# Channel product: upper remainders stacked over lower ones, with a new written order

## The chip, the cores and the metric

The kernel runs on one core of a Trainium2 chip. It uses TensorE (PE, its weight loads PEld), VectorE (DVE), ScalarE (ACT), GpSimd (POOL) and the SyncE queue (SP), from which the loads and stores are issued; transfers inside the core's memory are issued from POOL. The metric is the device time of one execution in microseconds. Before the change three timed runs gave 355.57 to 356.24 us, median 355.92.

## The reference

Two stages, one after the other. The first is a gated linear attention with a running state, over 4 batches, 8 heads, 768 tokens and head size 40:

```python
m_new = np.maximum(f_gate[:, :, t] + m, i_gate[:, :, t])
f_stab = np.exp(f_gate[:, :, t] + m - m_new)
i_stab = np.exp(i_gate[:, :, t] - m_new)
C = f_stab * C + i_stab * np.einsum('bhd,bhe->bhde', vt, kt)
n = f_stab * n + i_stab * kt
y = sigmoid(o_gate) * (C @ qt) / np.maximum(np.abs(n . qt), 1.0)
```

The second works on its result x, laid out as 4 batches x 768 tokens x 320 channels:

```python
theta = x @ w_theta
zr, zi = x * np.cos(theta), x * np.sin(theta)
y = einsum('ts,bsd->btd', w_tok_r, zr) + einsum('ts,bsd->btd', w_tok_i, zi)
u = x + y
out = u + np.maximum(u @ w_ch, 0.0)
```

The last line is the channel product. Weights arrive as 64-bit words and are decoded on the chip.

## The kernel before

Tokens are cut into 6 chunks of 128. A unit is one chunk of one batch: 24 units, numbered n = 4 * chunk + batch. Two batches make a pair `pr` (0 or 1); 12 pairs q = n // 2. A unit runs on TensorE as scores (`score`, L370), the products of weighted scores with the values (`pv`, L406 and L410) and a state product (`state`, L454). ACT makes the exponentials (`exps`, L389), POOL cuts them to a triangle (`select`, L393), and DVE multiplies them into the scores (`weigh`, L399; below, the unit's weighting). A unit's denominator (L417 to L424), its output gate (L430 or L432) and `head_out` (L439) give its part of X.

For each pair of units X is turned (L609), split into an upper part rounded to the fast 32-bit format and a lower remainder (L621, L625), and multiplied by `w_theta` (`angles`, L647). The angles are reduced (L655 to L671), sine and cosine are taken on ACT (L674, L675), multiplied by X (L684) and split into upper and lower parts of z (L687, L690). Five groups j of the token mix (L549, 12 products each for a pair and a chunk) add into `acc` (`gather`, L563). The token weights are decoded in 18 pieces of 512 columns (`split`, L263 to L285); four operations of a piece (L269 to L271, L275) run on DVE only, the others may go to ACT, DVE or POOL.

Every product of two such numbers takes three matmuls: upper by upper, lower weight by upper, upper weight by lower. The channel product (`channel`, L944 to L956) has 320 rows of contraction for a batch, 128 + 128 + 64. The two batches of a pair lie one behind the other in five tiles of 128 rows, so tile 2 holds the last 64 rows of the first batch in its upper half of partitions, and the first 64 rows of the second in its lower half. Output tiles jj = 0, 1 belong to the first batch, 3, 4 to the second, 2 to both. `ks_of` (L930) lists the parts of an output tile. They run in blocks of half the tokens (384 columns): a pair block for (0, 3) or (1, 4), and a single block for 2. In a pair block, 18 matmuls, the three half products of jj and the three of jj + 3 take turns, on the two halves of the partitions:

```python
products = [*x[:6], *(z for xy in zip(x[6:], y[:3]) for z in xy), *y[3:]]
```

There are 8 pair blocks of 18 matmuls and 4 single blocks of 15. The parts of u are `us[pr, k]`, upper and lower side by side, written by `u_hi` (L922) and `u_lo` (L925). The channel weights are decoded into two tiles, upper in `E_.w[0]` and lower in `E_.w[1]`, and rows that belong on the other half of the partitions are copied there by eight POOL transfers (`wch_copies`, L905). ReLU and sum are one DVE operation (`relu`, L967), then the store (L177).

What is computed is collected by `add` as numbered tasks with the engines that may run them; `issue` (L125) issues them in the order of `ORDER` (L47), a list written out by hand such as `934T`: task 934, on TensorE. V is DVE, A ACT, G POOL, D SP's loads and stores. Each engine works its tasks strictly in this order. Priorities and estimated times given to `add` play no part any more. The tasks 961 to 1028 are filling products on `ones` (L878), which keep TensorE busy; with a V behind their number they do nothing.

Of the kernel before, what the change touches and what calls it, by code (L numbers as in the profile page):

```python
# [10 lines left out]
F32R = mybir.dt.float32r  # L11
# [8 lines left out]
P = 128  # L20
# [13 lines left out]
WCOLS = 1792  # L34
PIECE = 512
# [17 lines left out]
117V 220V 108A 109A 173T 256D 161V 221V 162V 222A 230D 110V 239D 163A 118V 113G 174V 120T 223G 255D 225A 164V 111A
243G 175T 121V 180A 122V 980V 226V 240T 123A 231A 112V 124A 983T 227V 181T 176A 114A 232V 228A 305D 119A 370D 250A
254D 177V 115V 125V 135T 178V 260A 306D 182V 128G 179V 241V 183T 129V 244V 229G 233V 245T 371A 130V 184A 376D 372V
257D 186A 138A 251T 137A 234A 185V 261G 258T 126A 246V 136V 310A 324D 247V 323D 127V 131T 373V 235V 382D 304D 248A
259V 322D 147T 262V 318G 311G 374A 249V 133A 252A 263T 268V 963V 148V 375G 377A 132V 253V 134A 149A 378V 307D 150A
383A 187T 264A 328A 390D 384V 269T 188A 379V 308T 265V 270A 522D 189V 329G 985T 380A 312V 388D 190A 143T 309G 302D
191A 266V 381G 267V 271V 313T 385V 523A 192V 394A 524V 326T 408D 139T 314V 406D 525V 325D 315V 330V 395G 316A 389D
528D 144V 392T 140V 526V 193A 195V 145A 319T 194G 146A 396V 196A 272T 407D 142A 534D 410T 386A 456D 197V 141A 273A  # L60
988V 320V 214T 327V 412A 317V 387G 275V 321V 527G 331T 529A 215V 391D 274V 336A 530V 276T 458D 338A 474D 332V 999V
216V 989V 971V 333V 217A 531V 334G 337T 277A 393G 198T 335V 535A 457D 339V 413G 462A 278V 409D 536V 397T 532A 964V
279V 303A 974V 414V 463G 202T 476D 402G 674D 199V 200V 398V 201V 280A 411V 206T 399V 537V 204V 400G 203V 205V 460T
404A 281V 968V 284V 282A 210T 540D 208V 283G 454D 285A 992V 997V 464V 209A 680D 480A 403T 286V 478T 207V 533G 405V
401V 340T 459D 212V 415T 538V 211V 213V 675A 481G 341V 420A 990V 343V 539G 293T 342V 542D 416A 558D 676V 344T 482V
417V 1010V 294V 418G 546A 295V 544T 345V 290T 677V 461V 686D 678A 475D 346V 547G 422A 419V 421T 681A 679G 291V 347A
299T 292V 348A 682V 424T 301V 465T 470V 488A 548V 349G 300V 352G 423V 425A 562T 466V 687A 477D 426V 472A 287T 683V
353A 541D 467V 350A 427V 354G 455A 471T 970V 289V 428T 351G 473V 288V 543D 468V 479V 361T 995V 469V 559D 429A 560D
1007V 688V 684A 483T 554V 430V 545G 363V 431A 572G 965V 367T 484V 362V 564A 610D 485V 608D 490V 626D 975V 689V 489T
# [8 lines left out]
767G 764T 1021V 1002V 780D 836A 713D 585V 702A 644T 768V 588G 516T 844D 645A 761D 1025V 703V 589V 704A 707T 1012V
1011V 647V 782T 646V 779D 586A 590V 648T 587V 715G 705V 518V 969V 708G 719T 649V 517V 650V 1014V 841V 651A 600T 1027V
720V 709V 652A 721V 763D 967V 722A 653V 603T 602V 656G 601V 784A 846D 1018V 723V 758D 591T 605V 858D 726V 604V 765V  # L80
728T 593V 769T 592V 657A 785G 731V 774A 729V 837G 725T 658G 776A 597T 727V 654A 792G 759A 770V 730V 781D 655G 732T
# [964 lines left out]
```

## Time and profile before

| | before |
|---|---|
| timed runs, median (lowest to highest) | 355.92 us (355.57 to 356.24) |
| profiled execution, its own time | 357.73 us |
| its span, first to last instruction | 356.0 us |
| mean granted TensorE clock | 0.947 |
| PE, DVE, ACT, POOL busy | 325.5, 297.3, 220.5, 123.1 us |
| matmuls | 2286 |
| moved by DMA | 61.56 MB |

Busy time is the time in which at least one instruction of the engine was running; matmuls overlap, so a matmul's own duration is longer than the step from one to the next. The granted clock is 1.0 or 0.5 at any moment. "Idle before" a group names what released its first instruction.

### The profile page before, as it was taken

The numbers are of one execution on the slowest core, as the hardware profiler recorded it, in microseconds if no ns is written. First come the engines' busy times: TensorE is split into PE (matmuls) and PEld (weight loads), VectorE is DVE, ScalarE is ACT, GpSimd is POOL, SyncE is SP. The second block draws the span as 40 slices with busy tenths as digits, with TensorE's granted clock in tenths as the row PEclk, the third lists the DMA queues.
The fourth block names the chain that finished last, engine by engine and source line by source line (L and its number), as shares of the span: only waits on it lengthen the run. The fifth ranks groups of instructions, "written<-read, shape, count | busy, mean of one in ns | idle before, by whom it ended". The sixth has DMA issues, their size and how long they took to land.

```text
span 356.0 us, 6570 instructions
## 1 busy us (share of the span) xinstructions
PE 325.5 (91%) x2286; PEld 303.9 (85%) x2289; DVE 297.3 (84%) x629; ACT 220.5 (62%) x567; POOL 123.1 (35%) x111
## 2 busy tenths in 40 slices
PE   1487969979899999998999999999999999999995
PEld 1366959859799999997999989999999989998885
DVE  4998699786889998999989998798899998658632
ACT  2989788888979979596585838987850412201000
POOL 1223442323434636247352611614330092702000
PEclk9877676978999999999899999999999999999999
DMA  6965792996886764489627286346630021000155
GB/s 228 395 228 172 226 261 57 302 327 214 244 329 215 243 210 134 152 250 323 203 71 257 79 263 238 121 142 193 228 87 0 2 43 33 1 2 0 46 196 202
DMA packets 25164, 61.56 MB, mean 173 GB/s; under 512 B 3204, under 2 KB 11052, under 8 KB 25132
## 3 DMA queue, kind: packets, MB, share of 16 engines
q1 hardware_dynamic: 23915, 59.84, 51.1%
q0 software_dynamic: 1216, 1.31, 2.0%
q8 instruction: 18, 0.29, 0.3%
q14 instruction: 15, 0.11, 0.1%
HBM read 55.71 MB, written 4.12 MB: 168 GB/s over the span
## 4 chain that ended last, share of the span: by engine, by line
PE 63%; DVE 17%; DMA 12%; ACT 3%; POOL 2%; issue 2%; SPq 2%; DVEq 0%; POOLq 0%
PE pm L549 25%; PE pm L955 10%; PE pm L647 9%; PE ph L410 8%; DMA qk<-in_qk 5%; DMA eb<-e_d 4%; PE sc L370 3%; PE ph L406 3%; DVE acc L563 2%; PE pm L454 2%; DVE dt L399 2%; DMA q_t<-in_q 2%; DMA sg<-in_og 1%; DVE val L271 1%; DVE val L275 1%
## 5 line engine op out<-in xcount | busy, mean ns | idle before, releaser
L549 PE MATMUL pm<-w,z 128*128 128x384 f32 x600 | 112.2, 339 | 0.0
L549 PEld LDWEIGHTS pm<-w,z 128*128 128x128 f32 x600 | 103.4, 188 | 1.4 <-DVE acc L563 0.2
L563 DVE TENSOR_TENSOR acc<-pm,acc 128x384 f32<-128x384 f32 x100 | 52.1, 549 | 10.9 <-PE pm L549 10.6
L389 ACT ACTIVATE dt<-dt,bwT 128x128 f32<-128x128 f32 x160 | 49.0, 391 | 7.7 <-DMA dt<-g_d 7.6
L410 PE MATMUL ph<-tok_t,dt 128*128 128x41 f32 x384 | 49.4, 291 | 0.0
L410 PEld LDWEIGHTS ph<-tok_t,dt 128*128 128x128 f32 x384 | 48.5, 205 | 0.7 <-issue 0.2
L393 POOL TENSOR_SCALAR_AFFINE_SELECT dt<-dt 128x1024 f32<-128x1024 f32 (+1 forms) x26 | 29.3, 1130 | 49.6 <-ACT dt L389 37.5
L647 PE MATMUL pm<-wthp,xs 128*128 128x320 f32 (+1 forms) x216 | 38.3, 352 | 3.2 <-DVE xs L625 3.2
L647 PEld LDWEIGHTS pm<-wthp,xs 128*128 128x128 f32 (+1 forms) x216 | 30.7, 206 | 8.7 <-issue 4.8
L399 DVE TENSOR_TENSOR dt<-sc,dt 128x512 f32<-128x512 f32 x44 | 28.1, 680 | 1.4 <-PE sc L370 1.3
L955 PE MATMUL pm<-u,w 128*128 128x384 f32 (+1 forms) x112 | 28.4, 355 | 0.0
L370 PE MATMUL sc<-qk 64*128 64x128 f32 x352 | 26.5, 292 | 1.8 <-DMA qk<-in_qk 1.8
L370 PEld LDWEIGHTS sc<-qk 64*128 64x128 f32 x352 | 22.2, 193 | 5.2 <-issue 1.6
L690 POOL TENSOR_TENSOR z<-ab,z 128x640 fp32r<-128x640 f32 x8 | 12.8, 1603 | 35.8 <-DVE den L423 21.4
L549 PE MATMUL pm<-wsm,z 128*128 128x384 f32 x120 | 24.6, 359 | 0.0
L967 DVE SCALAR_TENSOR_TENSOR acc<-pm,acc 128x384 f32<-128x384 f32 x20 | 10.8, 555 | 14.5 <-PE pm L955 14.5
L549 PEld LDWEIGHTS pm<-wsm,z 128*128 128x128 f32 x120 | 22.2, 201 | 0.2
L406 PE MATMUL ph<-C,q_t 120*128 120x123 f32 x120 | 17.2, 279 | 5.2 <-DVE X L439 2.7
L406 PEld LDWEIGHTS ph<-C,q_t 120*128 120x128 f32 x120 | 15.4, 191 | 6.8 <-POOL q_t L484 3.0
L955 PEld LDWEIGHTS pm<-u,w 128*128 128x128 f32 (+1 forms) x112 | 17.6, 187 | 3.0 <-issue 3.0
L430 ACT ACTIVATE sg<-sg,den 128x40 f32<-128x40 f32 x72 | 16.7, 314 | 5.0 <-DVE den L424 5.0
L922 ACT CAST u<-acc 128x768 fp32r<-128x768 f32 x4 | 3.2, 834 | 26.4 <-DVE acc L563 21.5
(136 smaller groups left out, 603.8 us busy)
## 6 DMA issues: line engine op xcount, KB each, us to landing
qk<-in_qk SPq DMA_DIRECT2D x24, 512.0 KB
dt<-g_d SPq DMA_DIRECT2D x20, 512.0 KB
raw<-in_wtok SPq DMA_DIRECT2D x18, 512.0 KB
tok_t<-in_tok SPq DMA_DIRECT2D x24, 364.5 KB
sg<-in_og SPq DMA_DIRECT2D x12, 320.0 KB
q_t<-in_q SPq DMA_DIRECT2D x20, 180.0 KB
eb<-e_d SPq DMA_DIRECT2D x60, 60.0 KB
out<-acc SPq DMA_DIRECT2D x5, 384.0 KB
```

The source lines that it names most:

```text
L370: nc.tensor.matmul(u.sc[s][:, hp], u.qk[rows, 1, hp], u.qk[rows, 0, hp], start=True, stop=True)
L389: nc.scalar.activation(u.dt[:, h, :], src, AF.Exp, bias=bwT[:, c, r:r + 1])
L393: nc.gpsimd.affine_select(d, d, pattern=[[0, h1 - h0], [1, P]], compare_op=ALU.is_ge, fill=0.0, base=0, channel_multiplier=-1)
L399: nc.vector.tensor_mul(d2[:, s], u.sc[s], d2[:, s])
L406: nc.tensor.matmul(u.ph[:, gg * 3 * E1:(gg + 1) * 3 * E1], u.q3[:, gg, :], C[b][:, gg, :], start=(gg == 0), stop=False)
L410: nc.tensor.matmul(u.ph[:, h * E1:(h + 1) * E1], u.dt[:, i, :], v1(h, h + 1), start=(c == 0 and i == 0), stop=(i == H - 1))
L430: nc.scalar.mul(u.s3[:, h], u.s3[:, h], u.den[:, h])
L549: nc.tensor.matmul(pm[:, :TH], x.z[:, a, s, j * P:(j + 1) * P], w[x.c][:, b, s, th * TH:(th + 1) * TH], start=(k == 0), stop=(k == last))
L563: nc.vector.tensor_add(a, pm[:, :TH], a)
L647: nc.tensor.matmul(S_.th[b - b0][:, :DM], p.xs[a0:a1, a, k, :], wt5[a0:a1, s, k, :], start=(x == of(b)[0]), stop=(x == of(b)[-1]))
L690: ENG[e].tensor_sub(zv(1, s), trig(s), zv(0, s).bitcast(F32))
L955: nc.tensor.matmul(o.pm[jj][:, :TH], E_.w[s][a0:a1, col:col + P], us[pr, k][a0:a1, a, ts], start=(x == ones[jj][0]), stop=(x == ones[jj][-1]))
```

## The change

A new tile `both` is laid over `wt5`, the `w_theta` tile, which is free after the last angles. For each pair it holds, for the 64 remainder rows of either batch, the upper part of u on one half of the partitions and the lower part of the same rows on the other half. `hi_again` writes the upper parts from `acc` (two copies of 64x768, on DVE in the new order), `lo_across` moves the lower parts across (two POOL transfers). `wch_twice` places the upper weights of these rows, 256 columns, on both halves, in 512 more columns of `E_.w[0]` (four POOL transfers). One matmul over 128 rows of `both` then does upper by upper and upper weight by lower together. The lower weight by upper stays a 64-row matmul; the two of a pair block stand one behind the other. A pair block has 16 matmuls: six, one stacked, two of 64 rows, one stacked, six. Single blocks stay as they are.

The task list grows from 1118 to 1124: `wch_twice` twice (1051, 1052), and `hi_again` and `lo_across` behind tile 2's parts of each pair (1059, 1060 and 1092, 1093). Later numbers shift. `ORDER` is another list from its fourth load on. In it, among much else: the loads of the output gates (2, 4, 151) stand behind the heads of units 0 and 1; two more pieces of token weights are decoded before unit 0's weighting (73, 75); unit 0's output gate (79) is on ACT instead of POOL; ACT's order of table functions ahead of the first sine (109) is exp, sigmoid, exp, sigmoid, exp instead of exp, sigmoid, exp; of the filling products on TensorE three stand in the first tasks, 988, 977 and 984 (before: 966, 986, 976, 983, 985), and two, 1005 and 997, behind the last block; the last single blocks run before the pair blocks.

```diff
 ORDER = """
-0V 960G 1D 6D 17D 21D 2D 18D 19D 9D 10V 4D 12V 151D 7D 11G 8D 26A 13V 25D 27V 20D 14A 154D 24D 15T 28V 155T 56V 29A
-30A 32A 31V 16A 22T 156A 33V 58V 38A 69A 71A 81A 34V 59D 39V 23T 35A 36A 70G 98A 37V 966T 153D 40V 82T 73V 72G 43A 48D
...
+0V 960G 1D 6D 17D 18D 21D 19D 9D 8D 10V 25D 12V 20D 11G 13V 26V 14A 27V 32A 15T 155T 28V 33V 29A 30V 31V 34V 38A 16V
+35A 39V 22T 36A 156A 37V 84T 40V 69A 56V 48D 24D 154D 43A 2D 41A 44V 71A 23T 42V 45V 49A 72G 46A 218D 85A 50V 153D 4D
+47V 3A 51V 98V 224D 7D 58V 151D 87A 5A 70G 88G 73V 219A 81A 75V 57G 74T 220V 52A 76T 152A 60V 82T 77A 78V 61A 99T 53V
...
+1055A 1057V 899T 897V 898V 1056V 1061A 934T 900V 901V 1058G 1063A 1062V 820T 935A 1064V 936V 1060G 1083T 822V 937V
+998V 821V 938A 1059V 1081T 939V 965V 942V 940A 1084V 943A 1076T 941V 944V 948T 1077V 1078V 1082V 945T 949V 950V 954T
...
+1080D 1071D 1079D 1113T 1119V 1004V 1103T 1115V 1114V 1108T 1105V 1104V 1107D 1116D 1106D 1117D 1120D 1098T 1109V
+1110V 1112D 1111D 1005T 1099V 997T 1100V 1101D 1027V 1019V 1102D
 """.split()
...
-        E_.w = [wbig.tile([P, WCOLS], F32R, name="w"), const.tile([P, WCOLS], F32R, name="wsm")]
+        E_.w = [wbig.tile([P, WCOLS + WDUP], F32R, name="w"), const.tile([P, WCOLS], F32R, name="wsm")]
...
+    def wch_twice(half):
+        for to in range(2):
+            nc.gpsimd.dma_start(E_.w[0][64 * to:64 * (to + 1), WCOLS + 256 * half:WCOLS + 256 * (half + 1)],
+                              E_.w[0][64 * half:64 * (half + 1), 1408:1664])
+    ready += [add("G", 1.3, PAR["wch"], lambda half=half: wch_twice(half), ends) for half in range(2)]
+    both = wt5.rearrange("p a k e -> p (a k e)")[:, :4 * S].rearrange("p (r n t) -> p r n t", r=2, n=2)
...
+            def hi_again(e, pr=pr):
+                for n in range(2):
+                    rows = slice(64 * n, 64 * (n + 1))
+                    COPY[e](both[rows, pr, n], acc[rows, 5 * pr + 2, :])
+            def lo_across(pr=pr):
+                for n in range(2):
+                    nc.gpsimd.dma_start(both[64 * (1 - n):64 * (2 - n), pr, n], us[pr, 2][64 * n:64 * (n + 1), 1])
+            stacked = [add({"A": 1.4, "V": 0.9}, None, PAR[f"u{pr}"] + k, hi_again, [*p.done[k], *pairs[-1].theta]),
+                       add("G", 1.3, PAR[f"u{pr}"] + k, lo_across, [ul[-1], *pairs[-1].theta])]
...
-                        products = [*x[:6], *(z for xy in zip(x[6:], y[:3]) for z in xy), *y[3:]]
+                        c0 = js[0] * P
+                        twice = [(jj, 5 + n, WCOLS + 256 * n + c0, 0, P, 0, 0) for n, jj in enumerate(js)]
+                        lower = [(jj, 2, 1408 + c0, 64 * n, 64 * (n + 1), 1, 0) for n, jj in enumerate(js)]
+                        products = [*x, twice[0], *lower, twice[1], *y]
...
-                        nc.tensor.matmul(o.pm[jj][:, :TH], E_.w[s][a0:a1, col:col + P], us[pr, k][a0:a1, a, ts],
-                                         start=(x == ones[jj][0]), stop=(x == ones[jj][-1]))
+                        u = us[pr, k][a0:a1, a, ts] if k < 5 else both[:, pr, k - 5, ts]
+                        nc.tensor.matmul(o.pm[jj][:, :TH], E_.w[s][a0:a1, col:col + P], u,
+                                         start=(x == of(jj)[0]), stop=(x == of(jj)[-1]))
...
-                         [*ready, cleared, *ul_], bank=bank, banks=len(js), cols=384 * 15)
+                         [*ready, cleared, *ul_, *([ul[2], *stacked] if len(js) == 2 else ())], bank=bank, banks=len(js), cols=384 * 15)
```

More of the change, by code (lines that the diff above doesn't have):

```diff
@@ L34 @@
 WCOLS = 1792
+WDUP = 512
 PIECE = 512
@@ L53 @@
[L53 to L57, printed above, removed]
@@ L78 @@
[L78 to L81, printed above, removed]
-599V 845D 996V 598V 786V 850A 860D 977V 775T 848T 777V 859D 771V 510T 847D 783V 733A 772V 851G 773V 734V 787T 852V
@@ new lines @@
+114A 235V 257D 176A 124A 241V 374A 115V 260A 177V 382D 135T 306D 377V 304D 244V 178G 125G 302D 179V 268V 245T 378V
+126A 250A 375V 183T 379V 252A 251T 136V 261G 522D 985V 246V 184A 258T 138V 137V 310A 324D 128V 305D 131T 247V 322D
+185V 127G 323D 186V 259G 129A 380A 262V 187T 248A 130G 381G 134V 253V 383A 311G 987V 132V 523A 307D 133V 269T 249V
+188A 263T 384V 328A 524V 147T 318A 390D 389D 385V 270V 308T 189V 329G 149A 386A 148V 150A 139T 525V 388D 264A 190A
+265V 271V 309G 191A 312V 143T 325D 266G 336G 267V 140V 528D 394A 192V 313T 387V 193V 195V 326T 145V 402G 314A 408D
@@ new lines @@
+144V 142A 141V 320A 315V 272T 194G 330V 196A 319T 146A 273A 392T 407D 197V 316A 321V 327G 214T 275V 391D 395G 529A
+317V 526A 530V 406D 331T 412A 534D 274V 527G 217A 396V 303A 276T 413G 458D 332V 333V 975V 966V 990V 393V 531V 337T
+277A 334V 674D 410T 338G 456D 335V 278V 397T 216V 279A 215V 535V 532A 339V 280A 536V 409D 198T 457D 964V 537V 404A
+202T 281V 462A 398V 284G 201V 199V 200V 403T 411G 203V 204V 210T 475D 399V 474D 1002V 205V 533G 285A 476D 1018V 414V
+282A 206T 400A 286G 405V 459D 283V 213A 460T 212A 207V 675A 994V 973V 211V 401V 680D 208A 676V 340T 209A 538A 415T
@@ new lines @@
+487V 826D 363V 614A 566V 549T 433V 368V 976V 970V 689V 296T 563V 628D 832D 369V 626D 550V 551V 609D 436V 358T 434V
+437A 989V 435V 690A 552A 962V 992V 297V 438G 612T 298V 359V 555T 556A 553V 492T 691V 632A 567T 996V 360V 495V 557V
+633G 493V 611D 355T 574A 494V 615G 627D 568V 694D 569V 616V 573T 570G 827A 496T 622A 693D 357V 571V 575V 1014V 613V
+629D 630T 828V 497A 692D 617T 606D 356V 498V 833V 499V 448T 829V 618A 500A 1000V 834V 451T 979V 706V 830A 450V 501G
+607A 449V 634V 623T 504G 439T 711D 710D 624A 619V 505V 620A 453V 831G 696T 1012V 452V 441V 445T 506G 440V 502A 625V
@@ L929, in mlstm_mixer @@
             ul.append(add({"V": 0.87, "G": 1.76}, None, PAR[f"u{pr}"] + k, u_lo, [t], pick=PAR["ulo"][k % 2]))
+            if k != 2:
+                continue
+            def hi_again(e, pr=pr):
[7 more added lines that the diff above has]
+                       add("G", 1.3, PAR[f"u{pr}"] + k, lo_across, [ul[-1], *pairs[-1].theta])]
         def ks_of(jj):
             if jj < 2:
-                return [(0, jj * P, 0, P), (1, 704 + jj * P, 0, P), (2, 1408 + jj * P, 0, 64)]
+                return [(0, jj * P, 0, P), (1, 704 + jj * P, 0, P)]
             if jj > 2:
                 col = 64 + (jj - 3) * P
-                return [(2, 1408 - 64 + col, 64, P), (3, 384 + col, 0, P), (4, 1088 + col, 0, P)]
+                return [(3, 384 + col, 0, P), (4, 1088 + col, 0, P)]
             return [(0, 256, 0, P), (1, 960, 0, P), (2, 1664, 0, P), (3, 320, 0, P), (4, 1024, 0, P)]
```

66 lines of the change are left out of this document (29 added, 37 removed).

## The prediction

> **What bounds the kernel now.** I read the page first, then busy time by stretches of the span, the chain that ended last, and the weight loads of the channel product.
>
> ```profile
> span 356.0 us, 6570 instructions
> PE 325.5 (91%) x2286; PEld 303.9 (85%) x2289; DVE 297.3 (84%) x629; ACT 220.5 (62%) x567; POOL 123.1 (35%) x111
> ```
>
> The same execution by stretches; the columns are busy time and count of PE, PEld, DVE, ACT, POOL, then granted clock, DMA share and GB/s.
>
> ```profile
> ...
> 49.00:59.20 10.20, 9.16 (x44) 8.33 (x46) 9.40 (x17) 8.70 (x32) 3.78 (x4) 0.50 0.41 121
> ...
> 76.30:83.10 6.80, 6.80 (x30) 6.03 (x29) 4.32 (x10) 4.62 (x15) 2.09 (x2) 0.50 0.80 238
> ...
> 134.50:352.50 218.00, 214.93 (x1493) 203.37 (x1491) 182.53 (x382) 108.01 (x258) 75.04 (x63) 0.99 0.40 130
> ...
> ```
>
> From 134.5 us on TensorE is busy for 214.93 of 218.00 us at full clock: there, time changes only if its work changes, or if something arrives late. The early part is different: TensorE waits for others, and stretches run at half clock. The profiled execution took 357.73 us, 1.7 more than its span; the timed runs have a median of 355.92. I work out a difference on the profiled execution and take it off the median.
>
> **The products.** A pair block of the channel product has 18 products now. The chain shows it against 12 products of the token mix, of the same 128x384 output:
>
> ```profile
> 300.51 2.59 PE pm L647 x18
> 303.10 4.19 PE pm L549 x24
> 307.29 8.26 PE pm L955 x47
> ...
> 326.94 3.04 PE pm L955 x18
> 329.98 2.09 PE pm L549 x12
> 332.07 20.40 PE pm L955 x114
> ...
> 352.50 0.56 DVE acc L967
> ```
>
> A full product takes 2.09 / 12 = 0.174 us. The six half products overlap two by two, so a block is 12 + 3 = 15 slots, 2.61 us; it takes 3.04. What are the other 0.43 us? The weight loads (PEld) around the half products of a block:
>
> ```profile
> 333.05 0.19 PEld L955 LDWEIGHTS pm<-u,w 64*128 64x128 f32 x2 [0.24 <-issue]
> 333.16 0.19 PEld L955 LDWEIGHTS pm<-u,wsm 64*128 64x128 f32 x2
> 333.34 0.19 PEld L955 LDWEIGHTS pm<-u,w 64*128 64x128 f32 x2
> 333.78 0.19 PEld L955 LDWEIGHTS pm<-u,w 128*128 128x128 f32 x1 [0.25 <-issue]
> ```
>
> Pair follows pair 0.18 us later (333.16 to 333.34); the holes of 0.24 and 0.25 us are where 128 rows change to 64 and back. The loss belongs to the two edges of the half group, not to its length. After the change a block is 6 full + 1 full + 1 pair + 1 full + 6 full products: still 15 slots, still two edges. Worth zero by this reading. If instead the 0.43 us belonged to the three pairs, each would cost 0.14, two fewer would save 0.29 a block and 8 blocks 2.3 us. No row shows a pair alone between full products, so I keep both ends, -2.3 to 0, and take 0, since the holes stand at the edges only. The Trainium skill, "TensorEngine Tiling (Array Packing)", Tiling Modes / Key Properties, speaks against the change too: a change of tiling mode drains TensorE, a change of tile does not. It covers the case that no row shows, a pair alone, and gives 0 where the price per pair gives -2.3; the trace agrees as far as it goes, with its holes of 0.24 and 0.25 us.
>
> **What is added around them.** Four copies of 64x768 (`hi_again`) stand on DVE, four transfers (`lo_across`) and four more (`wch_twice`) on POOL's queue. Rows for the like, and for what runs beside them (start, duration; the last fence has min/median/max in ns):
>
> ```profile
> 297.04 0.56 DVE L922 CAST u<-acc 128x768 fp32r<-128x768 f32 x1
> ...
> 299.44 0.95 DVE L925 TENSOR_TENSOR u<-acc,u 128x768 fp32r<-128x768 f32 x1
> ...
> 303.55 0.88 DVE L661 SCALAR_TENSOR_TENSOR rr<-rr,pm 128x320 f32<-128x320 f32 x2
> ...
> 313.91 0.82 DVE L690 TENSOR_TENSOR z<-ab,z 128x640 fp32r<-128x640 f32 x1
> ```
>
> ```profile
> 305.29 0.74 ACT L674 ACTIVATE rr<-rr 128x640 f32<-128x640 f32 x1
> ```
>
> ```profile
> 315.38 6.42 PE L549 MATMUL pm<-w,z 128*128 128x384 f32 x36
> ```
>
> ```profile
> L907 POOL DMA_DIRECT2D w<-w x2: 544/565/586, 290.1 to 292.2; - x2
> ...
> DMA to landing us min/median/max: 2.0/2.1/2.2
> ```
>
> So 2 x 0.56 = 1.1 us of DVE and 2 x 0.57 + 2.1 = 3.2 us of transfer for each pair. `wch_twice` puts 4 x 0.57 = 2.3 us between the two weight copies on POOL, some 17 us ahead of the first channel product. For pair 0 the order then is angles, one mix group (2.09), two single blocks (2 x 2.61), the first pair block. Its eighth product, the first to read the new tile, is 2.09 + 5.22 + 7 x 0.174 = 8.5 us behind the angles. The transfer waits for the angles and lands 3.2 us after them; behind it POOL has nothing until pair 1's remainder. The copy is queued on DVE behind three remainder subtractions (3 x 0.95), the angles' fraction (0.88), a size and two gathers (about 0.5 each), and ends some 5 us behind the angles. Cover is over 3 us for both.
>
> The copy also stands ahead of the last z. Now z is ready at 313.91 + 0.82 = 314.73 and the last mix starts at 315.38: 0.65 us to spare. After, that mix comes 2.09 + 5.22 + 3.04 = 10.4 us behind the angles, where 4.19 + 8.26 = 12.4 us are now. z needs the 5 us to the copy's end, with the two sines (2 x 0.74) beside it, then on DVE four operations of 0.82 and an evaluation of 0.56: about 8.8. Spare about 1.6, worth zero; if something of 2 us more stands there, the difference shows.
>
> The end keeps its length: the last block is a pair block instead of a single one, but the same blocks are run, and behind the last product stand one evaluation (352.50, 0.56 us) and a store, as now. The two filling products now ordered last run beside that store.
>
> **The order of the start.** This is where the time can move. DVE's groups of the first 100 us, the last two numbers being mean ns and idle time before them, then ACT's:
>
> ```profile
> L271 DVE SCALAR_TENSOR_TENSOR val<-raw,val 128x512 int32<-128x512 int32 x10 | 7.9, 795 | 0.3
> L275 DVE SCALAR_TENSOR_TENSOR val<-raw,val 128x512 int32<-128x512 int32 x10 | 7.4, 743 | 0.0
> L269 DVE TENSOR_SCALAR val<-val 128x512 f32<-128x512 f32 (+1 forms) x12 | 6.4, 537 | 2.2 <-ACT val L263 2.2
> L270 DVE TENSOR_SCALAR val<-val 128x512 int32<-128x512 int32 (+1 forms) x12 | 5.1, 424 | 0.4
> L285 DVE TENSOR_TENSOR w<-val,w 128x512 fp32r<-128x512 f32 x3 | 2.5, 819 | 0.0
> L484 DVE TENSOR_TENSOR q_t<-q_t,eb 120x384 f32<-120x384 f32 x3 | 2.4, 814 | 3.0 <-DMA eb<-e_d 3.0
> L423 DVE TENSOR_SCALAR den<-den 128x8 f32<-128x8 f32 x7 | 1.8, 260 | 3.8 <-ACT den L417 3.8
> ```
>
> ```profile
> L263 ACT ACTIVATE val<-raw 128x512 f32<-128x512 f32 x10 | 6.8, 680 | 2.1 <-DMA raw<-in_wtok 2.1
> L430 ACT ACTIVATE sg<-sg,den 128x40 f32<-128x40 f32 x24 | 5.5, 313 | 0.4 <-DVE den L424 0.4
> L389 ACT ACT_TABLE_LOAD x3 | 3.8, 1283 | 0.1
> L284 ACT CAST w<-val 128x512 fp32r<-128x512 f32 x6 | 3.6, 623 | 0.5 <-DVE val L275 0.4
> ```
>
> A piece of token weights costs DVE 0.795 + 0.743 + 0.537 + 0.424 = 2.5 us. The new order decodes two more pieces ahead of unit 0's weighting: with their casts and subtractions about 6 us. I follow this to two points where TensorE waited.
>
> The first point is the start of the first mix group, at 59.39 (rows of ACT, PE and DVE in order of time):
>
> ```profile
> 46.23 0.47 ACT L674 ACTIVATE rr<-rr 128x320 f32<-128x320 f32 x1
> ```
>
> ```profile
> 57.62 0.61 PE L878 MATMUL pm<-ones 128*128 128x512 bf16 x1
> 58.45 1.18 PE L454 MATMUL pm<-tok_t 128*120 128x123 f32 x6 [0.22 <-issue]
> 59.39 2.33 PE L549 MATMUL pm<-w,z 128*128 128x384 f32 x12
> ```
>
> ```profile
> 72.44 1.28 DVE L399 TENSOR_TENSOR dt<-sc,dt 128x512 f32<-128x512 f32 x2
> ```
>
> Ahead of the first sine ACT gets unit 0's gate (8 x 0.313 = 2.5), three decode starts (3 x 0.68 = 2.0), two casts (1.2), copies of x (about 2) and two more table loads (exp, sigmoid, exp, sigmoid, exp: 2 x 1.28 = 2.6), and loses about 1.4: 9 us more. The sine moves from 46.2 to about 55, and z is ready some 3.5 us later. That is 58.5 against 59.39: no loss, and 0.9 us to spare, because now DVE's decode, not the sine, stands last there.
>
> The second is unit 5's weighting at 72.44, behind which TensorE's products of unit 5 stand. DVE ahead of it: one piece more (2.5), two subtractions moved from POOL (2 x 0.82), minus the query product (0.81) that goes to POOL; the small operations exchanged, none over 0.6 us, take off about 0.3. Sum **+3.0**. Waits on that way: the longest wait for `eb` stood before that query product and goes with it, half of its 3.0 us (**-1.5**); the waits for ACT's denominator, 3.8 us in two, lie behind 2.5 us of decode now, so I take off 2.4 (**-2.4**; 0 to 3.8). A new wait can come where DVE's pieces meet the added table load: 0 to 1.3, taken whole, since that load is in front of the piece's first operation in ACT's queue (**+1.3**). TensorE then has the angles of pair 1 (2.59) and unit 5's state product (0.6, half of the 1.18 at half clock) behind it instead of ahead, and one filling product less (about 0.4, from 0.61 at half clock), against one mix group more ahead (2.09): **-1.5**. Sum: 3.0 + 1.3 - 1.5 - 2.4 - 1.5 = -1.1 us.
>
> Loads: fewer bytes stand ahead of unit 0's heads, since the output gates moved back; but in SP's queue the third weight piece now stands ahead of unit 1's heads and waits for DVE to free a buffer, and the sixth stands ahead of the store of the gate sums. Those are needed some 5 us later than they land. Worth zero, up to 1 us if not. DMA from 134.5 on is 0.40 busy; no cost there.
>
> So -1.1 us: **354.8 us**, against 355.92.
>
> **Rivals.** (a) *The loss is per pair*: 2.3 us less, 352.5. For it: the 0.43 us; against: the even step inside the group. (b) *Warmer start*: if the wait behind the half-clock stretch 76.30 to 83.10 falls away, 6.80 us of work take 3.4: 351.4. The clock there is 0.50 though TensorE is full. The Trainium skill, "TensorE: Matmul & The Clock Gate", Part 1, has the clock go full after some 3.4 us of sustained work; the trace differs, with 0.50 for the 10.2 us from 49.00, where TensorE is busy 9.16. (c) *Slower*: decoding first pushes attention back and no wait goes away in return: 3.0 + 1.3 - 1.5 = +2.8, 358.7. It decides if unit 5's weighting starts later than about 73.5. For it: 9 us more on ACT ahead of the sine, 0.9 to spare, three filling products left at the start of five; against: DVE's queue holds less that must wait. (d) *Nothing moves*: the change saves no slot and the two orders come out level, 355.9.
>
> **How the numbers follow.** What this measurement can tell from no change is 0.2%, 0.7 us. Forecast (-0.7 to -3.5 us) 0.34, (a) 0.05, (b) 0.10, (d) 0.15, (c) 0.36. Faster 0.49, same 0.15, slower 0.36. Range: from 350, (b) with one more wait of 1.4 gone, to 360, (c) with the spare of the first mix group gone as well, 1.3 us. Of the likeliest case alone: 352.4 to 355.2.
>
> **What would show it.** Pair blocks still at 3.0 us with two holes of 0.24 in the weight loads (right), or 2.75 (then (a)). Last z ready before its mix, no idle TensorE behind 300 us. First mix group between 58 and 60.5 us, unit 5's weighting between 70 and 73; later, (c) holds. Two more table loads before the first sine. The forecast is wrong if the stretches of half clock before 100 us change in number, or if a wait for a transfer opens behind 100 us.

## The result, and the profile after

The changed kernel takes 345.78 us (median of four runs, 344.85 to 346.66) where the kernel before, on the same chip, took 355.75 (354.59 to 356.24): a ratio of 0.972, with a 95% interval of 0.969 to 0.976. The forecast was 354.8, in a range of 350 to 360. The profiled execution took 346.4 us. (Ratios here leave disturbed executions out; the kernel before spread over 350 to 362 us, and its medians from one set of executions to the next over 355.1 to 359.5.)

The head of the page after:

```profile
span 344.5 us, 6551 instructions
...
PE 316.2 (92%) x2270; PEld 296.1 (86%) x2273; DVE 293.0 (85%) x627; ACT 219.2 (64%) x561; POOL 125.6 (36%) x123
```

11.5 us of span are gone, though only 16 of 2286 matmuls are. The chain that ended last shows that the pair block has not become shorter: start, length, line and count, as in the prediction.

```profile
304.06 6.27 PE pm L550 x36
310.32 3.04 PE pm L983 x16
313.37 4.17 PE pm L550 x24
317.54 23.40 PE pm L983 x126
```

A pair block took 3.04 us with 18 products and takes 3.04 with 16. So the time must have come out of the order. Here is the first part of the span in stretches of 20 us, for the kernel before and then the changed one (busy time and count of PE, PEld, DVE, ACT, POOL, then granted clock, DMA share, GB/s):

```profile
0.00:20.00 20.00, 7.46 (x54) 6.56 (x56) 15.05 (x28) 12.01 (x36) 5.67 (x10) 0.87 0.88 322
20.00:40.00 20.00, 16.63 (x122) 14.28 (x121) 15.86 (x33) 17.38 (x50) 3.77 (x6) 0.76 0.55 159
40.00:60.00 20.00, 16.55 (x100) 14.96 (x101) 18.31 (x37) 17.92 (x56) 9.63 (x9) 0.69 0.69 195
60.00:80.00 20.00, 16.84 (x117) 15.43 (x116) 17.01 (x41) 17.70 (x53) 4.76 (x5) 0.91 0.94 300
80.00:100.00 20.00, 18.71 (x149) 16.91 (x148) 14.94 (x31) 17.64 (x45) 8.94 (x7) 0.92 0.77 248
```

```profile
0.00:20.00 20.00, 8.42 (x65) 7.45 (x65) 15.30 (x32) 10.46 (x26) 2.90 (x8) 0.90 0.77 279
20.00:40.00 20.00, 10.33 (x73) 9.13 (x76) 19.34 (x33) 19.15 (x48) 7.07 (x9) 0.58 0.74 228
40.00:60.00 20.00, 17.47 (x140) 15.48 (x139) 18.40 (x43) 19.86 (x59) 7.66 (x8) 0.93 0.85 264
60.00:80.00 20.00, 18.62 (x147) 16.97 (x146) 19.72 (x43) 19.40 (x67) 9.97 (x10) 0.99 0.88 293
80.00:100.00 20.00, 19.96 (x171) 18.67 (x169) 18.84 (x44) 18.33 (x46) 9.63 (x9) 1.00 0.74 227
...
134.50:341.00 206.50, 206.32 (x1432) 195.41 (x1431) 168.38 (x364) 100.85 (x241) 66.97 (x66) 1.00 0.44 138
```

Take the columns one by one. TensorE is idle in the first 100 us for 100 - 76.19 = 23.8 us before and 100 - 74.80 = 25.2 after: not less. Its clock is better: stretches of half clock made up 37.5 us before and make up 23.9 now, 20.5 of them in one piece (16.1 to 36.6), in which TensorE waits for 11.2 us anyway. The time in which it works at half clock fell from 34.5 to 12.4 us. VectorE is busy for 81.17 us before and 91.60 after: **its idle time in the first 100 us falls from 18.8 to 8.4 us, by 10.4**. And behind 134.5 us TensorE is busy for 206.32 of 206.50 us at full clock, where before it lost 3 us to waits and a step of half clock.

What VectorE waited for between 14.9 and 100 us, before and after (what waited for what, total us, times, longest):

```profile
DVE den L423 <- ACT den L417: 3.8, 2, 2.4
DVE q_t L484 <- DMA eb<-e_d: 3.0, 2, 1.5
DVE rr L661 <- ACT rr L655: 2.1, 2, 1.4
DVE dt L399 <- PE sc L370: 1.3, 1, 1.3
DVE rr L657 <- PE pm L647: 1.2, 2, 0.7
DVE val L269 <- ACT val L263: 1.2, 2, 1.0
```

```profile
DVE q_t L485 <- DMA eb<-e_d: 0.7, 1, 0.7
DVE dt L400 <- PE sc L371: 0.7, 2, 0.4
DVE val L270 <- ACT val L264: 0.5, 1, 0.5
DVE den L424 <- ACT den L418: 0.3, 1, 0.3
DVE rr L662 <- ACT rr L656: 0.3, 1, 0.3
DVE X L440 <- ACT sg L431: 0.2, 1, 0.2
```

12.6 us of waits have become 2.7; each of the old ones is shorter or gone. Two readings stood against each other: the gain is VectorE's idle time, or it is TensorE's clock. The experiments were to part them, and the order from the products.

### The profile page after: what moved, and what is told of

It reads as the page before. It is cut to its first block, busy times and chain, and to the rows that moved or that the text cites. A ratio compares the mean times of both kernels' runs of the same rounds, so it can differ in the third digit from the quotient of the medians.

```text
span 344.5 us, 6551 instructions
## 1 busy us (share of the span) xinstructions
PE 316.2 (92%) x2270; PEld 296.1 (86%) x2273; DVE 293.0 (85%) x627; ACT 219.2 (64%) x561; POOL 125.6 (36%) x123
## 4 chain that ended last, share of the span: by engine, by line
PE 78%; DVE 12%; issue 4%; DMA 3%; ACT 1%; POOL 1%; SPq 1%; DVEq 0%; ACTq 0%; POOLq 0%
PE pm L550 33%; PE ph L411 10%; PE pm L983 10%; PE pm L648 8%; PE sc L371 6%; PE ph L407 4%; PE pm L455 3%; PE pm L610 2%; DMA eb<-e_d 2%; DVE val L272 1%; DVE val L276 1%; DMA z<-in_wth 1%; DVE val L271 1%; ACT dt L390 1%; DVE wsm L208 1%
## 5 line engine op out<-in xcount | busy, mean ns | idle before, releaser
L411 PE MATMUL ph<-tok_t,dt 128*128 128x41 f32 x384 | 47.1, 284 | 12.1 <-DVE dt L400 11.2
L411 PEld LDWEIGHTS ph<-tok_t,dt 128*128 128x128 f32 x384 | 46.4, 198 | 12.8 <-DVE dt L400 11.5
L394 POOL TENSOR_SCALAR_AFFINE_SELECT dt<-dt 128x1024 f32<-128x1024 f32 (+1 forms) x26 | 27.8, 1074 | 37.8 <-ACT dt L390 36.7
L648 PE MATMUL pm<-wthp,xs 128*128 128x320 f32 (+1 forms) x216 | 35.1, 329 | 1.8 <-DVE xs L626 1.6
L648 PEld LDWEIGHTS pm<-wthp,xs 128*128 128x128 f32 (+1 forms) x216 | 27.3, 187 | 7.6 <-issue 4.6
L983 PE MATMUL pm<-u,w 128*128 128x384 f32 x80 | 22.5, 338 | 0.0
L433 POOL TENSOR_TENSOR sg<-sg,den 128x320 f32<-128x320 f32 x12 | 9.6, 798 | 34.1 <-DVE den L425 30.1
L448 ACT ACTIVATE tok_t<-tok_t,bwT 128x40 f32<-128x40 f32 x90 | 20.7, 317 | 0.0
L286 POOL TENSOR_TENSOR w<-val,w 128x512 fp32r<-128x512 f32 x10 | 13.7, 1374 | 18.6 <-ACT w L285 17.2
L656 ACT ACTIVATE rr<-pm 128x320 f32<-128x320 f32 x17 | 7.0, 432 | 19.7 <-PE pm L648 19.7
L691 POOL TENSOR_TENSOR z<-rr,z 128x640 fp32r<-128x640 f32 (+1 forms) x8 | 12.6, 1576 | 18.9 <-ACT z L688 18.5
L485 POOL TENSOR_TENSOR q_t<-q_t,eb 120x384 f32<-120x384 f32 x11 | 13.1, 1192 | 12.7 <-DMA eb<-e_d 12.7
```

The costliest lines, as they stand in the source:

```text
L286: t = add({"G": us * 2, "V": us}, None, prio, lambda e: ENG[e].tensor_sub(lo(), T.v, hi().bitcast(F32)), [t], pick=PAR["wlo"])
L394: nc.gpsimd.affine_select(d, d, pattern=[[0, h1 - h0], [1, P]], compare_op=ALU.is_ge, fill=0.0, base=0, channel_multiplier=-1)
L411: nc.tensor.matmul(u.ph[:, h * E1:(h + 1) * E1], u.dt[:, i, :], v1(h, h + 1), start=(c == 0 and i == 0), stop=(i == H - 1))
L448: nc.scalar.mul(k4[:, g, j], k4[:, g, j], by[:, g, j:j + 1])
L648: nc.tensor.matmul(S_.th[b - b0][:, :DM], p.xs[a0:a1, a, k, :], wt5[a0:a1, s, k, :], start=(x == of(b)[0]), stop=(x == of(b)[-1]))
L983: nc.tensor.matmul(o.pm[jj][:, :TH], E_.w[s][a0:a1, col:col + P], u, start=(x == of(jj)[0]), stop=(x == of(jj)[-1]))
```

## The experiments

**1. Products and order, one at a time.** First the kernel before with nothing but the new order:

```
-ORDER = OLD
+ORDER = [x for x in NEW if x not in (1051G, 1052G, 1059V, 1060G, 1092V, 1093G)]
```

with the numbers behind those six counted down again.

> The kernel before with nothing but the new order (the six new tasks left out of it; pair blocks keep their 18 products). Theory 'order': the pair block is 3.04 us in both traces, so the products are worth nothing and this kernel takes 345.8 us, ratio 0.972, like the changed one. Rival 'loss per pair': 2.3 us of the gain belong to the products, and it takes 348.1, ratio 0.979.

Measured: 346.79 us (345.25 to 347.62), ratio 0.979 (0.974 to 0.983). Then the new products in the old order:

```
-ORDER = NEW
+ORDER = OLD + (1051G, 1052G, 1060G, 1059V, 1092V, 1093G)
```

with the six put in behind the first weight copies, and behind the last remainders that they read.

> The changed kernel in the order of before; only the six new tasks are put into it (weight copies behind the first of the old ones, copy and transfer of each pair behind its remainder). Theory 'order': 355.8 us, ratio 1.000, pair blocks of 3.04 us. Rival 'loss per pair': 353.5, ratio 0.994, pair blocks of 2.75 us.

Measured: 358.55 us (351.23 to 360.99) beside 355.46 (353.01 to 361.73); ratio 0.994 (0.988 to 1.001). Neither theory's number is excluded by that. Its trace also has a wait that neither named: TensorE stands for 1.6 us ahead of the channel product behind a gathering operation, and a step of half clock follows at 308.8 us. The copy was put where the new order doesn't have it, so this run says only that the products bring no gain of 10 us. What they are worth the next comparison settles better, on one chip with the changed kernel:

> The changed kernel once more, on one chip with the next three, as their common base: 345.8 us.

> The kernel before with nothing but the new order, beside the changed kernel. The traces have both kernels' pair blocks at 3.02 us: theory 'products worth nothing', within 0.5 us of the changed kernel. Rival 'the 1.0 us between the two medians so far belongs to the products': 1 us or more above it.

Measured: 345.12 us (344.99 to 345.74) and 346.09 (345.30 to 347.14). The 1.0 us between the two came out again, as large as the rival had it, but the traces don't show it in the products: in these profiled runs the stretch from the first channel product to the start of the last block, all blocks but one, lasts 42.13 us in the changed kernel (295.01 to 337.14) and 42.14 with the old products (296.10 to 338.24). The 1.1 us by which the latter is late there it has from the start, where the two kernels are alike: a mix group that begins at 105.84 in the one begins at 106.88 in the other, which had half clock from 53.2 to 63.4. Half clock doesn't explain all of it, though: the five executions of the changed kernel with a mean clock of 0.965 have a median of 345.12, the four with the old products and the same mean clock one of 345.98. So **the blocks show no gain from the products, and nearly all of it is the new list's**: 9.7 us (355.76 to 346.09); up to 0.9 us stays open. The list is more than an order. In it 151 tasks, filling tasks aside, also run on another engine, and with the old products VectorE's busy time falls from 297.3 to 289.7 us. No run here parts the order from the choice of engines.

**2. Which part of the order.** Four kernels with the old products take the order of one list up to a cut and that of the other behind it. By the time at which their tasks are done the cuts stand for "new to 94 us", "old to 104 us", "new to 70 us" and "old to 70 us" (in these lines a task is the same task on whatever engine):

```
-ORDER = OLD
+ORDER = NEW[:332] + [x for x in OLD if x not in NEW[:332]]
+ORDER = OLD[:341] + [x for x in NEW if x not in OLD[:341]]
+ORDER = NEW[:236] + [x for x in OLD if x not in NEW[:236]]
+ORDER = OLD[:230] + [x for x in NEW if x not in OLD[:230]]
```

> Before's products; the first 332 tasks in the new order (in the changed kernel TensorE is through with them at 94.1 us), all others in the order of before. Before had TensorE through with nearly the same tasks at 102.6. Theory 'two gains that add up': 8.5 us are won in the start and stay, 347.3 us, ratio 0.976; TensorE has its waits of 1.8 and 0.6 us behind 134.5 us still. Rival 'one whole': the lead runs into VectorE's queue, which is full up to about 210 us, and more waits open behind 100 us: 351 us or more, ratio above 0.986.

> Before's products; the first 341 tasks in the order of before, all others in the new order. Theory 'two gains that add up': the new order's part behind the cut takes 250.4 us where before's takes 253.4, so 352.8 us, ratio 0.992: no wait of 1.8 us and no half clock behind 134.5 us. Rival 'one whole': the later part without its lead wins nothing, 355.8, ratio 1.000, or it wins more than 3 us, and then the lead was not the main thing.

> Before's products; the first 236 tasks in the new order (VectorE is through with them at 69.7 us in the changed kernel), all others in the order of before. Theory 'VectorE's idle time in the first 100 us is what the span carries': up to the cut VectorE was idle for 7.1 us in the changed kernel; from the cut to 100 us the order of before brings its own 18.8 - 11.9 = 6.9, together 14.0, 4.8 less than before, so 351 us where before takes 355.8. Theory 'the clock': by 70 us the new order has lost 6 us of TensorE's time to half clock, that of before 12; 349.5 if all of it counts. Rival 'only the later half of the start counts': 355.8.

> Before's products; the first 230 tasks in the order of before (VectorE through with them at 70.5 us), all others in the new order. Theory 'VectorE's idle time': 11.9 us up to the cut as before and the new order's 8.4 - 7.1 = 1.3 behind it, together 13.2, 5.6 less, so 350.2 us. Theory 'the clock': the half clock at 76.3 goes, no other: 354. Rival 'only the first half of the start counts': 355.8.

Measured: new to 94 us 350.07 (348.38 to 354.45), ratio 0.985 (0.980 to 0.990); old to 104 us 356.96 (350.99 to 360.44), ratio 1.000 (0.994 to 1.005); new to 70 us 352.55 (350.78 to 354.32), ratio 0.995 (0.991 to 0.999); old to 70 us 354.34 (352.13 to 355.90), ratio 0.998 (0.994 to 1.002). So the start brings more than half of the gain by itself (355.5 - 350.1 = 5.4 us), the rest without this start nothing, and both together 8.7 (346.79). "Two gains that add up" is wrong: behind an old start other waits open. With the old order to 70 us VectorE was idle for 18.3 us in the first 100, not for the 13.2 that I had added up from the two traces; a wait of 3.8 us for the pieces' sizes from ScalarE was new. A stretch of an order doesn't take its idle time along into another list. What held in all four is the relation of the measured idle time to the span; it is in the table below.

**3. The clock.** The kernel before, with four filling tasks more in TensorE's waits, none longer than its wait in the trace of before:

```
-    for x in [oned] * 8 + warm_after:
+    more = iter([2, 2, 2, 8, 14, 2, 12, 2, 8])
+    for x in [oned] * 8 + warm_after:
...
-            for k in range(2):
+            for k in range(next(more)):
```

In the order 962T stands ahead of 170T, 963T of 120T, 964T of 263T and 968T of 567T.

> The kernel before with four filling tasks more, put on TensorE ahead of four of its waits: 8 products ahead of unit 3's spreading (wait 1.97 us at 29.7), 14 ahead of the second half of the first angles (3.23 at 46.6), 12 ahead of unit 5's products (2.67 at 71.6), 8 ahead of unit 13's products (1.76 at 164.2). Each is shorter than its wait at full clock, by 0.215 us a product, so no work is held up. Theory 'the waits are paid twice, the second time as half clock': the stretches of half clock at 31.9, 49.0, 76.3 and 168.5 go; the late one is worth 1.7 us, that at 76.3 up to 3.4: 350.7 us, ratio 0.986, and down to 345 if the two early ones count in full. Rival 'the clock does not hang on these waits': the stretches stay, 355.8 or some tenths more. Rival 'VectorE sets the start': the stretches before 100 us go but TensorE waits longer instead, 354, ratio 0.995.

Measured: 355.04 us (351.28 to 359.56) beside 355.07; ratio 1.000 (0.993 to 1.006). Its stretches, columns as above:

```profile
20.00:40.00 20.00, 17.80 (x112) 14.03 (x113) 14.12 (x27) 14.74 (x41) 3.48 (x5) 0.66 0.49 144
40.00:60.00 20.00, 17.01 (x132) 13.65 (x133) 16.86 (x37) 19.29 (x60) 10.17 (x9) 1.00 0.82 216
60.00:80.00 20.00, 15.99 (x106) 14.15 (x107) 18.86 (x43) 16.35 (x49) 4.96 (x4) 0.91 0.74 265
80.00:100.00 20.00, 20.00 (x168) 17.77 (x168) 16.41 (x34) 18.89 (x51) 8.12 (x7) 1.00 0.79 253
```

Half clock fell from 37.5 us to 17.1, less than the changed kernel has, and the stretches at 49.0, 76.3 and 168.5 are gone. The time did not move. VectorE's idle time in the first 100 us is 18.7 us, as before: its queue still waits, now 5.8 us of it for denominators. That looks like the rival "VectorE sets the start", and against rival (b) of the prediction, by which the clock would have brought 4.5 us or more. But the run does not decide it, because the fills (L879) did not stay inside the waits:

```profile
74.51 0.48 DVE L439 TENSOR_TENSOR X<-ph,sg 128x320 f32<-128x320 f32 x1
75.88 2.75 PE L879 MATMUL pm<-ones 128*128 128x512 bf16 x11 [2.37 <-DVE acc L567]
78.47 0.83 PE L406 MATMUL ph<-C,q_t 120*128 120x123 f32 x6
```

Unit 5's products (L406), which before followed the end of L439 within 0.2 us, now start 3.5 us behind it (74.99 to 78.47): the fill ahead of them waited for a buffer itself and then held them up. The fill ahead of unit 3's spreading held that up from 34.8 to 37.8 us, with its input there since 33.2. In the whole span the fills took 9.9 us more of TensorE than those before (13.2 less 3.3), and its idle time gave only 3.7 of them (30.5 to 26.8). TensorE's work at half clock fell from 34.5 to 16.4 us, but the fills used up what that could bring. Within this kernel the time does go with the clock: of ten executions those at a mean clock of 0.989 and 0.967 took 351.3 and 359.6 us, and the correlation over all ten is -0.95. So what a higher clock alone is worth stays open here. The fills in the changed kernel:

> The changed kernel with three filling tasks more: 30 products in TensorE's wait of 11 us ahead of unit 0's products (29.45 us), 6 and 4 ahead of the second half of the first angles and of unit 3's products. Theory 'clock': half clock at 29.8 to 36.6 and 57.1 to 60.5 goes, TensorE saves 4.4 us of its time there; what of it reaches the end is up to VectorE. Theory 'the start is VectorE's': it is busy for 9.5 of each 10 us there, so less than 1 us reaches the end, 345 us. Theory 'the start is TensorE's': 341.5 us, ratio 0.960. If the clock stays at half through the filling, the products end 1.7 us late: 347.

Measured: 344.81 us (344.57 to 345.04). TensorE's idle time in the first 100 us fell from 25.2 to 14.3 us and its half clock from 23.9 to 13.7 us; the time by about 1 us against another chip's 345.78, VectorE's idle time by 0.5. But the half clock that went had lain over waits: at half clock TensorE was busy for 12.4 us without these fills and for 12.8 with them. Half clock over a wait costs next to nothing, then; this run does not show what it costs over work.

**4. Dead work on one engine each.** In the changed kernel, at 46 to 49 us, through a filling task, moved there, that does nothing otherwise:

```
+            if nf == 5:
+                for k in range(12):
+                    nc.vector.tensor_mul(ones, ones, ones)
```

The second kernel has ten times `nc.scalar.copy(ones, ones)` in its place, the third that filling task on TensorE with 28 products.

> The changed kernel with dead work on VectorE: 12 multiplications of the 128x512 tile of ones by itself (about 0.3 to 0.6 us each, so 4 to 7 us; the trace gives the sum) ahead of the piece decoded at 45.6 us. The start is idle on VectorE for 2.5 us between there and 100 us. Theory 'VectorE paces the first 100 us': the time grows by the dead work less at most these 2.5 us; for 6 us that is 349.3 to 351.8. Theory 'TensorE and its clock pace it': TensorE takes the delay up in its own waits and loses one or two steps of half clock at most: 346 to 348.

> The changed kernel with dead work on ScalarE: 10 copies of the 128x512 tile of ones, about 0.6 us each, at 47 us. Theory 'VectorE paces the first 100 us, ScalarE only feeds it': much less than the 6 us arrives, under 3 us, 346 to 348.8, as far as pieces and denominators wait in ScalarE's queue. Rival 'ScalarE paces it' (9.9 of 10 us busy there as well): 350 to 352.

> The changed kernel with dead work on TensorE: one filling task of 28 products, 6 us at full clock, ahead of unit 2's products at 45.8 us. TensorE is idle for 3.9 us between there and 80 us and loses 1.7 us to half clock. Theory 'VectorE paces the first 100 us': some of the 6 us goes into these waits, 0 to 3 us arrive, 346 to 349. Theory 'TensorE paces it': nearly all arrives, 350 to 352.

The dead work's groups on VectorE and on ScalarE, from the two traces:

```profile
L878 DVE TENSOR_TENSOR ones<-ones 128x512 bf16<-128x512 bf16 x12 | 6.0, 498 | 0.4
```

```profile
L878 ACT COPY ones<-ones 128x512 bf16<-128x512 bf16 x10 | 6.2, 617 | 0.3
```

Measured: 352.56 us (351.20 to 352.80), 353.09 (352.57 to 353.31) and 353.88 (352.68 to 354.54); 6.8, 7.3 and 8.1 us above 345.78, though on another chip. My theory had VectorE's work arrive and the other two be taken up for the greater part. That fell: **6 us arrive in full, wherever they are put**. My reading is that at 45 to 60 us the three engines hand one chain to each other, and none has slack. More than the 6 us arrives, and there the clock has a part: with the dead work on VectorE and on ScalarE, TensorE's work at half clock rose from 12.4 to 23.5 and 22.8 us. And if 6 us more on TensorE arrive in full, so should time that TensorE loses to half clock in this stretch. But it shows how ScalarE's and TensorE's delay arrives: VectorE's idle time in the first 100 us went from 8.4 to 16.3 and 16.2 us. So VectorE is not the one cause. It is a place where every delay of the start can be counted.

**The count.** For the profiled run of each kernel: its span; VectorE's idle time in the first 100 us (100 less its busy time in the stretches; dead work counted as idle); the difference; and for comparison TensorE's idle time there and the length of all half clock, without the stretch at the very end, with TensorE's busy time at half clock behind it.

| kernel | median | span | VectorE idle | span less that | TensorE idle | half clock (busy in it) |
|---|---|---|---|---|---|---|
| before | 355.75 | 356.0 | 18.8 | 337.2 | 23.8 | 37.5 (34.5) |
| new products, old order | 358.55 | 355.4 | 17.1 | 338.3 | 23.1 | 34.1 (32.1) |
| before, filled | 355.04 | 355.0 | 18.7 | 336.3 | 21.9 | 17.1 (16.4) |
| old to 70 us | 354.34 | 353.8 | 18.3 | 335.5 | 24.4 | 34.1 (31.2) |
| old to 104 us | 356.96 | 352.1 | 17.6 | 334.5 | 22.0 | 23.9 (23.3) |
| dead work, TensorE | 353.88 | 351.4 | 16.2 | 335.2 | 26.0 | 27.3 (14.2) |
| dead work, ScalarE | 353.09 | 351.3 | 16.3 | 335.0 | 28.3 | 37.5 (22.8) |
| new to 70 us | 352.55 | 351.1 | 13.6 | 337.5 | 24.1 | 30.7 (18.5) |
| dead work, VectorE | 352.56 | 350.8 | 10.4 + 6.0 | 334.4 | 27.8 | 41.0 (23.5) |
| new to 94 us | 350.07 | 348.6 | 10.9 | 337.7 | 23.2 | 30.7 (18.5) |
| new order, old products | 346.79 | 344.8 | 9.7 | 335.1 | 23.6 | 30.7 (18.4) |
| changed | 345.78 | 344.5 | 8.4 | 336.1 | 25.2 | 23.9 (12.4) |
| changed, filled | 344.81 | 342.9 | 7.9 | 335.0 | 14.3 | 13.7 (12.8) |

The spans lie 13 us apart, the differences in the fifth column 4; TensorE's idle time shows no such order. Of the 11.5 us between the kernel before and the changed one, 10.4 are VectorE's idle time in the first 100 us and 1.1 the rest.

A second count can be set beside it, TensorE's own. In the kernel before, 16 products of L410 take 3.54 us at half clock (from 52.14 us) and 1.88 at full clock (from 43.32). So about half of what TensorE works at half clock is lost, an estimate of 17.3 us before and 6.2 in the changed kernel: 11.1 of the 11.5 us. In the ten kernels without added products on TensorE the span less this loss lies between 335.6 and 341.8 us; VectorE's count for the same ten lies between 334.4 and 338.3, and it holds in the other three too. VectorE's is the closer count, but the two are two books of the same start, not two gains to be added. Neither says what drives the other, and that stays open.

The relation is a count, not a law of the chip: from about 100 us on TensorE has work almost without a break in all of these, and when it gets there hangs on when VectorE has decoded, weighted and gathered enough.

**5. What the edges cost.** The prediction put the 0.43 us of a pair block down to the two edges of the half group. So the half products were made full ones: the lower weights of tile 2 stand twice, each time with zeros in the other 64 rows.

```
-        E_.w = [..., const.tile([P, WCOLS], F32R, name="wsm")]
+        E_.w = [..., const.tile([P, WCOLS + 256], F32R, name="wsm")]
...
     def wch_twice(half):
+        if half:
+            nc.scalar.copy(E_.w[1][64:P, WCOLS:WCOLS + 256], E_.w[1][64:P, 1408:1664])
+            for k in range(2):
+                nc.scalar.activation(E_.w[1][0:64, WCOLS + P * k:WCOLS + P * (k + 1)], ident[0:64, :], AF.Copy, scale=0.0)
+                nc.scalar.activation(E_.w[1][64:P, 1408 + P * k:1408 + P * (k + 1)], ident[64:P, :], AF.Copy, scale=0.0)
...
+                        lower = [(jj, 2, (1408, WCOLS)[n] + c0, 0, P, 1, 0) for n, jj in enumerate(js)]
                         products = [*x, twice[0], *lower, twice[1], *y]
```

> The changed kernel, with the two half products of a pair block as two full ones: the lower weights of each output stand in a tile of their own with zeros in the other 64 rows. 16 full products instead of 14 full and 2 half ones, no change between 128 and 64 rows. Theory 'the loss belongs to the two edges': a block takes 16 x 0.174 = 2.78 us instead of 3.04, eight blocks 2.1 us less than the changed kernel, 343.7. Rival 'the loss is something else': 16 slots and 0.43 us, 3.21 a block, 347.1.

> Full products in place of the half ones, beside the changed kernel: eight blocks of 2.80 us instead of 3.02, 1.8 us below it.

Measured: 344.59 us (343.60 to 344.99), and beside the changed kernel's 345.12 on one chip 343.52 (343.19 to 344.71), 1.6 us less; ratio to before 0.974 (0.969 to 0.978). The weight loads around the group of a pair block, in the changed kernel and in this one:

```profile
331.54 0.19 PEld L983 LDWEIGHTS pm<-u,w 128*128 128x128 f32 x1
...
332.59 0.19 PEld L983 LDWEIGHTS pm<-wthp,w 128*128 128x128 f32 x1
333.02 0.19 PEld L983 LDWEIGHTS pm<-u,wsm 64*128 64x128 f32 x2 [0.25 <-issue]
333.40 0.19 PEld L983 LDWEIGHTS pm<-wthp,w 128*128 128x128 f32 x1 [0.19 <-issue]
...
334.56 0.19 PEld L983 LDWEIGHTS pm<-u,w 128*128 128x128 f32 x1
```

```profile
332.24 0.19 PEld L989 LDWEIGHTS pm<-u,w 128*128 128x128 f32 x1
...
333.28 0.19 PEld L989 LDWEIGHTS pm<-wthp,w 128*128 128x128 f32 x1
333.47 0.36 PEld L989 LDWEIGHTS pm<-u,wsm 128*128 128x128 f32 x2
333.82 0.19 PEld L989 LDWEIGHTS pm<-wthp,w 128*128 128x128 f32 x1
...
335.05 0.19 PEld L989 LDWEIGHTS pm<-u,w 128*128 128x128 f32 x1
```

From the first weight load of one block to that of the next are 334.56 - 331.54 = 3.02 us, and 335.05 - 332.24 = 2.81 with one product more and no hole. Eight times 0.21 is 1.7 us; 1.6 were measured. With the fills as well:

> The changed kernel with the full products in place of the half ones and with the three filling tasks in the start. If the two are independent, the gains against 345.8 add up: 1.2 and 1.0 us, 343.6; the pair block 2.79 us. If the fills only move the start's waits about, 344.6 as with the full products alone.

> Full products and the three filling tasks in the start, beside the changed kernel: 1.8 us for the products and 0.5 us less of VectorE's idle time in the first 100 us, 2.3 us below it.

Measured: 343.12 us (342.86 to 344.95), and beside the changed kernel 343.36 (342.99 to 345.25): the best of all, 1.8 us below it, though of that the fills' part, 0.2 us, can't be told from nothing.

## Why the prediction was wrong, point by point

**The products: right.** Taken at zero, with the loss at the two edges. A single pair between full products keeps its holes (0.25 and 0.19 us above), and taking the edges away brought 1.6 us. Rival (a), a loss per pair, is out. The Trainium skill's rule in "TensorEngine Tiling (Array Packing)", Tiling Modes / Key Properties, that a change of tiling mode drains TensorE, agrees with the case that no row had shown before the change.

**What was added: right, in the order that came with it.** Behind 100 us TensorE has one wait, of 0.2 us, and none for a tile of u or z. That the cover belongs to the order the new products in the old order show, with their wait of 1.6 us.

**The start: the points came early or close, and the sum over them was not the gain.** From the changed kernel's rows in order of time (first sine, first mix group, unit 5's weighting and products):

```profile
53.36 0.47 ACT L675 ACTIVATE rr<-rr 128x320 f32<-128x320 f32 x1
...
57.48 3.75 PE L550 MATMUL pm<-w,z 128*128 128x384 f32 x12
...
69.60 1.28 DVE L400 TENSOR_TENSOR dt<-sc,dt 128x512 f32<-128x512 f32 x2
...
73.18 0.90 PE L407 MATMUL ph<-C,q_t 120*128 120x123 f32 x6
```

Two more table loads stand ahead of the first sine, as said; the sine comes at 53.4 (forecast: about 55), the first mix group at 57.5 (58 to 60.5), unit 5's weighting at 69.6 (70 to 73), and unit 5's products start 1.1 us earlier than before (74.27). That this is the forecast's number is luck: the sum had the weighting 0.4 us later (3.0 + 1.3 - 1.5 - 2.4), and it came 2.8 us earlier. The angles of pair 1, which the sum took as 2.59 us moved ahead of unit 5's products, had taken 4.7 us at half clock behind them; now they are through by then (69.63 to 72.44). **The step that failed is the sum of the start**: "+3.0" for VectorE's work moved ahead of unit 5, less 3.9 for two kinds of wait, with half clock left as it was.

Its terms for the waits were mis-sized. 9.9 us of VectorE's waits between 14.9 and 100 us went (12.6 less 2.7), where the sum held 3.9 (1.5 for `eb`, which went by 2.3; 2.4 for `den`, which went by 3.5) and 1.3 of a new wait that did not come (the pieces' wait for ScalarE fell from 1.2 to 0.5). The waits for the angles' fraction (3.3 us, to 0.3) were not looked at, since they lie behind the point where I stopped or beside it. Against them stood work that is moved ahead on an engine and is missing behind; by VectorE's count that is no loss to the end as long as the engine goes on without a break. And the sum had no term for the clock, which it left to rival (b); but TensorE's work at half clock fell by 22.1 us, a loss of some 11.1 us less. Which of these two drives the other stays open; the sum had neither in full. Had the forecast taken the 12.6 us of VectorE's waits as what an order can win, its lower bound would have been 355.9 - 12.6 = 343.3.

**Behind 134.5 us: wrong, by an amount that stays open.** I took 214.93 of 218.00 us as full and at full clock, and let it stay. The three us of waits there, one of them with a step of half clock behind it (168.5 to 171.9), are gone. What these are worth alone is not shown: with the old start the new rest won nothing (ratio 1.000), with the new start 3.3 us (350.07 to 346.79).

**Rival (b), the clock: the observation was right, the mechanism stays open.** Half clock did fall away at 76.3 and elsewhere, and the prediction's own sign of being wrong came true: the four stretches of half clock before 100 us became two. For the clock as the cause stand the second count and the -0.95 of experiment 3; against it, that VectorE's count is the closer one. No run took half clock alone away from TensorE's work; the fills added work of their own. What is shown is that half clock under a long early wait, as the new order has it, costs next to nothing. **Rival (c)** was to decide by unit 5's weighting later than 73.5; it came at 69.6. **(d)** fell with the result.

## What to carry to other kernels

Where an order is changed in a stretch in which several engines wait for one another, don't follow one milestone: sum the idle time of the fullest engine over the whole stretch up to where the bounding engine has unbroken work, and take that as what the order can win or lose; beside it, count what the bounding engine works at a lower clock. A fill that is shorter than a wait in the old trace can still hold up work in the new one: see there whether it ended before the input of the next product came. And a half group of products between full ones costs its two edges, with one pair in it as with three; a product padded with zeros can be cheaper.

## What the runs showed of the hardware

TensorE's clock changes in steps of 3.413 us. In the 15 profiled runs other than those of the last comparison on one chip, all 40 stretches of half clock ahead of the last products are whole multiples of that, one to seven steps long. 37 of the 40 began behind two steps in which TensorE had been busy for 0.77 or less on average; but more than twenty other steps with as little behind them were granted full clock, so that is no sufficient rule. The Trainium skill, "TensorE: Matmul & The Clock Gate", Part 1, has a free-running window of 3413 ns; the traces agree with this length. By the same place one busy window brings the full clock back; here the three steps from 31.9 us in the kernel before stayed at half with TensorE busy for 0.99 to 1.00 of each, so the measurement differs.

The steps lie elsewhere in each execution: the changed kernel's half clock was at 16.1 to 36.6 and 57.1 to 60.5 in one profiled run, and at 14.8 to 38.7 alone in the other. I take this for the reason why one and the same kernel with many waits, the one before, spreads over 350 to 362 us (mean clock 0.932 to 0.980, correlation with the span -0.72 over the 76 executions measured beside the experiments), where the changed one stays within 344.9 to 346.7; it is argued from that correlation, not shown by a run.
